# One 96-row load for each of queries, keys and factors, with constant rows below them, and a new list of the work

## The chip, the cores and the metric

The kernel runs on one core of a Trainium2 chip. The metric is the time of one execution on the device, in microseconds. A core has five engines that run side by side, each through its own list of instructions in order: PE (matrix products), VectorE (DVE in the profile), ScalarE (ACT), GpSimd (POOL) and SyncE (SP), which here issues nearly all transfers. An engine waits where an instruction needs what another engine or a transfer has not finished.

## The reference

Two blocks follow each other. The first is a gated linear attention: for each of 4 batches and 8 heads a 48x48 state runs over 768 tokens. Its output, with the heads side by side, is `x` of a second block: a Fourier mix over tokens and channels, a normalisation and two dense layers (384 to 1536 to 384).

```
f = 1.0 / (1.0 + np.exp(-f_logit))
for t in range(S):
    state = f[:, :, t, :, None] * state + np.einsum('bhd,bhe->bhde', k[:, :, t], v[:, :, t])
    y[:, :, t] = np.einsum('bhd,bhde->bhe', q[:, :, t], state)
...
X = np.fft.fft(x, axis=1)
X = np.fft.fft(X, axis=2)
u = x + np.real(X)
un = (u - mu) / np.sqrt(var + 1e-06)
return u + np.maximum(un @ w_ch1, 0.0) @ w_ch2
```

## The kernel before

**Units.** Two heads of one batch make a unit; there are 16 units, four to a batch. A unit's queries, keys and factors (`f_logit`) lie with channels on partitions and tokens along the row, 112 partitions in all: head 0 at 0 to 47, head 1 at 64 to 111. The 16 partitions between, 48 to 63, hold a copy of some rows so that vector work can run over all 112 at once; `FILL` takes in these rows where 64 outputs are wanted, `ROWS` leaves them out. The source rows of both heads follow each other, so `load` (lines 197 to 213) writes 96 rows to partitions 0 to 95 (line 212), which holds head 0, then the first 16 rows of head 1 as filling, then head 1's last 32 rows, and with a second transfer (line 213) 16 rows to partitions 96 to 111, so that 64 to 111 hold head 1 whole. Values come in two transfers (lines 206 and 207).

**Steps of a unit** (`attention`, then `outputs` and `fold`), one for each time that its number stands in the list: 1 exponential and logarithm of the factors on ScalarE (lines 372, 373); 2 a running sum on VectorE (379, 380); 3 exponentials of the sum on ScalarE (383, 384, 387); 4 queries and keys multiplied by them on VectorE (391, 392); 5 products of keys and queries in blocks of 64 tokens on PE (400); 6 their causal mask on VectorE (404); 7 first products with the values and the far blocks (559, 576, 579); 8 the rest of these and the state increments `ds` (599); 9 the state's running sum on VectorE (607); 10 products of states and queries (616) and copies out of PSUM (625 to 629); 11 the turn to tokens on partitions (636, 640, 641); 12 and 13 the folding for the Fourier transform (663 to 687). `K` with a unit's number turns its keys (538, 540).

**The other block.** `F` steps through the Fourier mix of a batch, `H` through its normalisation, `P` through the two dense layers. For batch 0 the first layer is plain products (`up`, line 865) and the first pair of token blocks also has a plain second layer (`po`, line 874). All later ones use fast matrix schemes with fewer products (lines 836 to 845 and 888 to 922), which need sums of weight blocks (`B`, `W`). The dense weights arrive as 64-bit floats in 24 pieces (`r` fetches one, `R` three) and are turned into 32-bit ones (`C`, lines 281 to 285: one step on ScalarE, two on VectorE, one on GpSimd). `V` and `c` read all of them again for a check. `D` is a group of eight matmuls whose result nobody reads (line 192).

**Order.** `ORDER` (line 27) is a list of such words; the loop over it (line 951 on) records each step, and every engine runs its part of the steps in the order recorded, SP's transfers too. A buffer that is loaded again makes SP wait until its last reader is done, and everything behind on SP waits with it. There are two to four buffers each for factors, keys and queries: units 2 and 3 use parts of the large tile `wide_t`, which from unit 8 on serves other ends. A transfer also waits for one that was issued eight before it. Unit 0's first use in the list:

```
"Z I D L0f 0 i D L2f 2 D L1f D 1 L0q 0 L0k r D D D L1q 1 0 D D L0v L1k 0 L2q 2 C D 0 0 L2k 1 D D r 0 "
```

`L0f` loads unit 0's factors, `L3fk` the factors and keys of unit 3, `0` takes unit 0's next step, `i` loads an identity matrix, `Z` and `I` set constants on GpSimd, `T` and `S` load and sort tables of cosines and sines.

Of the kernel before, what the change touches and what calls it, by code (L numbers as in the profile page):

```python
# [12 lines left out]
C = 128  # L13
# [2 lines left out]
HIGH = 22.0  # L16
SMALLEST = 1.125 * 2.0 ** -15
WARM = 2.0 ** 57
X_MIN = -24.0


# [3 lines left out]


ORDER = (
    "Z I D L0f 0 i D L2f 2 D L1f D 1 L0q 0 L0k r D D D L1q 1 0 D D L0v L1k 0 L2q 2 C D 0 0 L2k 1 D D r 0 "
    "L3fk K0 D 1 1 K1 1 C 0 0 r 2 2 L1v D 3 D D r L3q 0 L2v L4fk 3 K2 C 1 0 C 1 1 3 2 1 D 2 3 3 4 2 0 L3v "
    "1 2 L5fk 5 D D 3 4 R 2 1 5 2 3 K3 C 4 3 L4qv 3 T D 2 L6fk 3 L5qv 5 C 4 D 2 4 4 3 3 4 S 2 3 C 5 K4 4 "  # L30
    "F0 F0 4 F0 F0 r C K5 5 6 r C 4 L6qv 5 F0 r r 4 5 L7fk H0 H0 r 5 H0 C 6 C 5 P0 7 P0 P0 r 6 C L7qv 6 "
    "P0 P0 5 C 6 K6 P0 r 6 7 C r P0 C P0 r r 7 C P0 F0 6 5 7 r r L9fk B C P0 P0 6 C 6 r r K7 C F0 P0 7 C "
    "7 C r 6 r H0 r C P0 P0 C 7 6 C P0 L8fk 7 H0 B L8qv 9 P0 P0 H0 B B 9 P0 8 7 P0 B 8 P0 9 B P0 P0 P0 8 "
    "P0 7 L9qv 4 9 9 K9 P0 B P0 5 8 P0 P0 7 H0 9 P0 7 9 8 B 9 H0 6 P0 P0 L11fk 9 11 W P0 6 P0 P0 9 K8 P0 "
    "P0 P0 B P0 P0 P0 P0 P0 8 7 P0 P0 P0 F1 P0 F1 L11qv P0 F1 F1 11 8 F1 P0 8 8 L10fk 10 P0 P0 P0 8 10 H1 "
    "P0 L10qv B P0 11 P0 P0 10 10 H1 B P0 P0 11 10 K10 P0 10 B 10 11 K11 11 L12fk B P0 H1 B B P1 P1 P1 P1 "
    "P1 B P1 P1 P1 P0 P1 P1 P1 P1 F1 P1 P1 F1 P1 P1 10 12 9 12 10 P1 P1 10 8 L12qv H1 9 P1 P1 12 12 10 P1 "
    "P1 H1 11 P1 12 11 H1 12 11 P1 P1 P1 H1 P1 P1 P1 P1 L13fk 13 P1 11 H1 P1 P1 P1 P1 P1 P1 P1 8 P1 P1 12 "
    "K12 L14fk 13 P1 14 P1 P1 12 L13qv 13 11 10 P1 13 12 10 P1 K13 11 P1 P1 P1 P1 P1 P1 14 P1 12 P1 11 P1 "
    "P1 P1 F2 F2 P1 14 P1 L14qv 14 F2 P1 P1 F2 P1 13 13 F2 13 K14 F2 F2 L15fk 13 13 P1 14 13 H2 P1 15 P1 "  # L40
    "15 P1 P1 L15qv 15 14 P1 14 P1 H2 14 15 H2 14 P1 P2 P2 P2 P2 H2 P2 P2 P2 P2 P2 P2 P2 P2 P2 P2 P2 13 "
    "14 15 H2 15 V 13 P2 K15 15 14 15 H2 V 14 15 P2 V P2 14 15 12 P2 P2 P2 15 12 c P2 H2 V P2 P2 P2 P2 P2 "
    "c 15 15 P2 P2 F3 F3 F3 P2 F3 P2 H2 P2 c P2 F3 P2 P2 F3 P2 c V F3 P2 P2 V P2 P2 P2 c c V V P2 P2 P2 "
    "H3 c P2 H3 P2 P2 P2 c P2 H3 P2 P2 P2 P2 P2 P2 P2 P2 V P2 P2 V P2 P2 P2 P2 V P2 P2 P2 c P2 c V c P2 V "
    "P3 c V P2 P3 P3 H3 V H3 P3 P3 P3 P3 P3 H3 P3 P3 P3 P3 P3 P3 P3 c V c c P3 c P3 V V P3 P3 P3 c P3 P3 "
    "P3 P3 P3 V P3 P3 H3 P3 P3 P3 P3 c c P3 V V V P3 P3 V P3 P3 P3 c c P3 P3 P3 P3 P3 P3 c V P3 P3 H3 c "
    "P3 c P3 P3 P3 M P3 P3 P3 P3 P3 P3 P3 P3 P3 P3 P3 P3 P3 P3 P3 P3 P3 P3 P3 P3"
)


# [33 lines left out]
def kernel(  # L84
# [13 lines left out]
    nc = tc.nc  # L98
    B, HP, _, D, _, S = qkf.shape
# [6 lines left out]
    HD = DM // 2  # L106
    QS, QD = S // 4, DM // 4
    R = 64 + D
    ROWS = [slice(64 * r, 64 * r + D) for r in range(2)]

    FILL = [slice(0, 64), slice(64, 64 + D)]

    PLACES = [slice(0, C), slice(2 * C, 3 * C), slice(C, 2 * C)]

# [18 lines left out]
    wide_t = fixed([128, 5 * S + 4], "wide")  # L133
# [33 lines left out]

    place = const.tile([128, B, 4], U32, tag="place", name="place")

    def start():  # L170

        for t in g_t:
            nc.gpsimd.memset(t[:, S:], 0.0)
        nc.gpsimd.memset(bound, HIGH)
        nc.gpsimd.memset(bound.rearrange("p (c t) -> p c t", t=C)[:, :, 0:1], LOW)
        nc.gpsimd.memset(low, LOW)
        nc.gpsimd.memset(eps, 1e-6)
        nc.gpsimd.memset(two, 2.0)
        for t in te_t:
            nc.gpsimd.memset(t, 0.0)  # L180
        nc.gpsimd.memset(causal, 1.0)
        for s in range(2):
            half = causal[64 * s:64 * s + 64, :64]
            nc.gpsimd.affine_select(out=half, in_=half, pattern=[[1, 64]], compare_op=ALU.is_ge, fill=0.0,
                                    base=0, channel_multiplier=-1)

    started = []

# [9 lines left out]
    def load(u, *names):  # L198
        if u >= B * HP:
            return  # L200
        b, hp = divmod(u, HP)
        for name in names:
            if name == "v":
                v_of[u] = (p3.tile([128, NCH, 2 * D], F32, tag="v", name=f"v{u}"),
                           pr.tile([128, NCH // 2, 2 * D], F32, tag="vx", name=f"vx{u}"))
                nc.sync.dma_start(out=v_of[u][0], in_=v[b, hp])
                nc.sync.dma_start(out=v_of[u][1][64:], in_=v[b, hp, :64, 3:])
                continue
            t, i = home(name, u), "qkf".index(name)
            rows = qkf.rearrange("b h r d i s -> (b h r d) i s")  # L210
            first = 2 * D * u
            nc.sync.dma_start(out=t[:2 * D, :S], in_=rows[first:first + 2 * D, i])
            nc.sync.dma_start(out=t[2 * D:R, :S], in_=rows[first + D:first + 64, i])

    def tables():

# [316 lines left out]
    kT_of = {}  # L533
# [8 lines left out]
    def outputs(u, x_all, AT, Q, K, te, T=None):  # L542
# [12 lines left out]
        def values(c, r, rows, t, weights, moved=False):  # L555
            g, o, vals = into(c, r), (c % 3 if moved else c) * 2 * D + r * D, vxf if moved else vf
            new = (c // 3, g) not in opened
            opened.add((c // 3, g))
            nc.tensor.matmul(y[FILL[g], c // 3, c % 3 * C + t.start:c % 3 * C + t.stop],  # L559
                             lhsT=vals[rows, o:o + (64 if g == 0 else D)], rhs=weights,  # L560
                             start=new, stop=True, skip_group_check=True)

# [32 lines left out]
        for c in range(NCH - 1):  # L595
            for r in range(2):

                n = 1 if c < NCH - 2 else 2
                nc.tensor.matmul(ds[FILL[r], :, c:c + n], lhsT=kT_of[u][:, c, FILL[r]],  # L599
                                 rhs=vt[:, c, r * D:(r + 1) * D].unsqueeze(2).to_broadcast([128, D, n]),  # L600
                                 start=True, stop=True)
        yield
# [10 lines left out]
        yield  # L613

        for c, r in ((1, 0), (4, 1), (4, 0), (1, 1), (2, 0), (3, 1), (3, 0), (2, 1), (5, 0), (5, 1)):
            nc.tensor.matmul(y[ROWS[into(c, r)], c // 3, c % 3 * C:c % 3 * C + C], lhsT=st[ROWS[r], :, c - 1],  # L616
                             rhs=Q[ROWS[r], c * C:(c + 1) * C], start=False, stop=True,
                             skip_group_check=True)

# [330 lines left out]
    with tc.manual_schedule():  # L950
        for word in ORDER.split():
            kind, n = word[0], int("0" + "".join(c for c in word if c.isdigit()))
            if kind.isdigit():
                if n not in units:
                    units[n] = attention(n, lambda b=n // HP: x_all(b))
                next(units[n], None)
            elif kind == "K":
                keys_turned(n, home("f", n)[:R, :S])
            elif kind == "F":
                if n not in fronts:  # L960
                    fronts[n], rest[n] = fnet(n, x_of[n]), projected(n, x_of.pop(n))
                next(fronts[n], None)
            elif kind == "P":
                next(rest[n], None)
            elif kind == "W":
                combine()
            elif kind == "B":
                weight_sum()
            elif kind == "H":
                next(behind[n], None)  # L970
            elif kind == "r":
                fetch()
            elif kind == "V":
                reread()
            elif kind == "D":
                busy()
            elif kind == "C":
                weights()
            elif kind == "c":
                sizes()  # L980
            elif kind == "R":
                fetch(3)
            elif kind == "L":
                load(n, *word.strip("L0123456789"))
            elif kind == "I":
                start()
            elif kind == "i":
                nc.sync.dma_start(out=ident, in_=ident_in)
            elif kind == "T":
                wave = tables()  # L990
            elif kind == "S":
                sort_tables(wave)
            elif kind == "Z":
                zeros()
            elif kind == "M":
                flag = judge()
# [3 lines left out]
    with tc.If(again > 0):  # L1000
# [5 lines left out]
                nc.sync.dma_start(out=dst, in_=src[:, cols])  # L1006
        combine()
        nc.sync.dma_start(out=causal.rearrange("p (i n) -> p i n", n=32), in_=sel)
        for u in range(4):
            load(u, *("fkqv" if u < 3 else "qv"))  # L1010
        for b in range(B):
# [77 lines left out]
```

## Time and profile before

| | us |
|---|---|
| median of 3 runs | 530.24 (527.37 to 530.46) |
| the profiled execution | 528.67 |
| its span, first to last instruction | 526.9 |
| PE busy | 497.4 |
| VectorE busy | 379.6 |
| ScalarE busy | 224.8 |
| the `D` matmuls in PE's time | 14.4 |

The profile is of one execution. The span lies 1.8 us below its time, and the execution 1.6 us below the median. The groups of instructions give busy time, the mean of one in ns, and the idle time of the engine just before, with what ended it. Instructions on PE overlap, so its busy time doesn't mean that it runs at its peak. Slices are 13.2 us each.

### The profile page before, as it was taken

What the parts mean: (1) busy time and instruction counts of PE and PEld (TensorE: products, weight loads), DVE (VectorE), ACT (ScalarE), POOL (GpSimd) and SP (SyncE); (2) the same over time, 40 slices, a digit from 0 to 9 for tenths busy, and PEclk for the clock granted to TensorE, in tenths of its full rate; (3) what the DMA queues carried; (4) which work ended last, traced back from release to release, by engine and by line L of the source; (5) the groups of instructions that cost most, each with busy time, mean ns of one, the idle gap of its engine ahead of it and who ended that gap; (6) DMA issues with size and microseconds to landing.
All of it is one profiled execution on the core that took longest, in us unless ns stands there. A gap on an engine that the chain in (4) does not pass through costs nothing.

```text
span 526.9 us, 13784 instructions
## 1 busy us (share of the span) xinstructions
PE 497.4 (94%) x5854; PEld 456.9 (87%) x5854; DVE 379.6 (72%) x746; ACT 224.8 (43%) x529; POOL 58.0 (11%) x85
## 2 busy tenths in 40 slices
PE   4867789999999999999999999999999999999995
PEld 4756668866899889999999889999899999999995
DVE  3777998998896258696598886686787566757561
ACT  6474667655530371444634534451441405132230
POOL 3110633351001000100001000000000000010000
PEclk9788899999999999999999999999999999999998
DMA  8998635674021121103031212110323112421101
GB/s 212 258 242 214 188 106 159 193 214 124 12 76 63 39 70 44 43 1 117 23 89 51 55 55 71 47 63 14 106 61 104 47 61 91 145 66 60 34 1 36
DMA packets 20462, 48.15 MB, mean 91 GB/s; under 512 B 3366, under 2 KB 5991, under 8 KB 20391
## 3 DMA queue, kind: packets, MB, share of 16 engines
q1 hardware_dynamic: 19142, 43.43, 29.5%
q0 software_dynamic: 1104, 3.54, 1.8%
q8 instruction: 48, 0.79, 0.6%
q14 instruction: 24, 0.19, 0.1%
q10 hardware_dynamic: 144, 0.20, 0.1%
HBM read 42.44 MB, written 4.72 MB: 89 GB/s over the span
## 4 chain that ended last, share of the span: by engine, by line
PE 81%; DVE 9%; issue 1%; ACT 1%; DVEq 0%
PE ub L836 24%; PE fx L888 16%; PE fz L888 12%; PE up L865 7%; PE z L725 3%; PE po L874 3%; PE y L559 3%; PE mix L744 2%; PE pt L783 2%; PE ds L599 2%; DVE w L284 2%; PE y L616 2%; PE yt L636 1%; PE sc L400 1%; PE st L538 1%
## 5 line engine op out<-in xcount | busy, mean ns | idle before, releaser
L843 DVE TENSOR_TENSOR h<-h,ub 128x512 f32<-128x512 f32 x81 | 55.1, 686 | 40.4 <-PE ub L836 40.3
L692 POOL DMA_INDIRECT out_dram<-x,place x16 | 17.8, 1112 | 383.5 <-DVE x L918 261.6
L841 ACT ACTIVATE h<-ub 128x512 f32<-128x512 f32 x54 | 32.2, 597 | 58.6 <-PE ub L836 58.1
L865 PE MATMUL up<-unT,w 128*128 128x256 f32 x216 | 49.3, 381 | 0.6 <-ACT unT L784 0.6
L845 ACT ACTIVATE h<-h 128x512 f32<-128x512 f32 x54 | 33.9, 631 | 33.3 <-DVE h L843 33.3
L888 PE MATMUL fx<-block,h 128*128 128x192 f32 x264 | 46.6, 327 | 0.0
L836 PE MATMUL ub<-unT,w 128*128 128x128 f32 x360 | 46.6, 280 | 0.0
L865 PEld LDWEIGHTS up<-unT,w 128*128 128x128 f32 x216 | 40.2, 190 | 6.3 <-ACT unT L784 0.8
L888 PE MATMUL fx<-w,h 128*128 128x192 f32 x264 | 45.4, 327 | 0.0
L836 PEld LDWEIGHTS ub<-unT,w 128*128 128x128 f32 x360 | 43.2, 191 | 0.7
L888 PEld LDWEIGHTS fx<-block,h 128*128 128x128 f32 x264 | 43.3, 190 | 0.1
L888 PEld LDWEIGHTS fx<-w,h 128*128 128x128 f32 x264 | 42.7, 190 | 0.3 <-ACT unT L784 0.2
L836 PE MATMUL ub<-wide 128*128 128x128 f32 x288 | 39.0, 281 | 0.0
L836 PE MATMUL ub<-wide,w 128*128 128x128 f32 x288 | 38.2, 280 | 0.0
L285 POOL TENSOR_TENSOR w<-w,raw 128x384 uint32<-128x384 uint32 x24 | 27.2, 1132 | 75.9 <-DVE w L284 39.1
L836 PEld LDWEIGHTS ub<-wide 128*128 128x128 f32 x288 | 34.6, 191 | 1.0 <-issue 0.4
L836 PEld LDWEIGHTS ub<-wide,w 128*128 128x128 f32 x288 | 34.3, 191 | 1.1 <-DVE h L843 0.3
L379 DVE TENSOR_TENSOR_SCAN W<-g,bound 112x768 f32<-112x768 f32 x12 | 21.0, 1750 | 9.2 <-ACT g L373 9.2
L784 ACT COPY unT<-pt 128x384 f32<-128x384 f32 x24 | 11.6, 487 | 35.8 <-PE pt L783 35.8
L867 ACT ACTIVATE h<-up 128x256 f32<-128x256 f32 x36 | 13.5, 380 | 30.3 <-PE up L865 30.3
L559 PE MATMUL y<-at,v 64*48 64x64 f32 (+1 forms) x768 | 19.3, 229 | 6.6 <-DVE at L404 2.9
L559 PEld LDWEIGHTS y<-at,v 64*64 64x64 f32 (+1 forms) x768 | 15.6, 135 | 10.3 <-issue 4.1
(188 smaller groups left out, 1003.0 us busy)
## 6 DMA issues: line engine op xcount, KB each, us to landing
raw<-in_w_ch_dram SPq DMA_DIRECT2D x24, 384.0 KB, 6.1
v<-in_v_dram SPq DMA_DIRECT2D x16, 288.0 KB, 4.5
k<-in_w_ch_dram SPq DMA_DIRECT2D x12, 384.0 KB, 3.7
g<-in_w_ch_dram SPq DMA_DIRECT2D x12, 384.0 KB, 3.4
k<-in_qkf_dram SPq DMA_DIRECT2D x14, 288.0 KB, 4.0
g<-in_qkf_dram SPq DMA_DIRECT2D x12, 288.0 KB, 6.4
q<-in_qkf_dram SPq DMA_DIRECT2D x12, 288.0 KB
wide<-in_qkf_dram SPq DMA_DIRECT2D x10, 288.0 KB, 5.4
```

What stands on the lines that cost most here:

```text
L285: nc.gpsimd.tensor_tensor(bits, bits, lo, ALU.add)
L379: nc.vector.tensor_tensor_scan(W, g, bound[:R], 0.0, ALU.add, ALU.min)
L559: nc.tensor.matmul(y[FILL[g], c // 3, c % 3 * C + t.start:c % 3 * C + t.stop], lhsT=vals[rows, o:o + (64 if g == 0 else D)], rhs=weights, ...
L692: nc.gpsimd.indirect_dma_start(out=out.rearrange("b s d -> (b s) d"), out_offset=bass.IndirectOffsetOnAxis(ap=place[:, b, i:i + 1], axis=0 ...
L725: nc.tensor.matmul(z[:, cols], lhsT=src[:, j, lo:hi], rhs=tab[:, t, T % 2, cols], start=(i == 0), stop=(i == len(parts) - 1), skip_group_c ...
L836: nc.tensor.matmul(banks[bank][:, m * 128:(m + 1) * 128], lhsT=block(w)[:, m * 128:(m + 1) * 128], rhs=tokens(a), start=(new and m == 0), ...
L841: nc.scalar.activation(out, got, AF.Copy, scale=1.0 if how == "=+" else -1.0)
L843: nc.vector.tensor_tensor(out, out, got, ALU.add if how == "+" else ALU.subtract)
L845: nc.scalar.activation(out, out, AF.Relu)
L865: nc.tensor.matmul(pp[:, :256], lhsT=w1[:, kt, m * 128:(m + 1) * 128], rhs=unT[:, kt], start=(kt == 0), stop=(kt == 2))
L874: nc.tensor.matmul(po[:, :DM], lhsT=h[:, m, t], rhs=w2[:, m], start=(m == 0), stop=(m == NF - 1))
L888: nc.tensor.matmul(out, lhsT=h[:, m], rhs=blocks[i][:, m], start=(start and m == 0), stop=(m == H - 1), skip_group_check=True)
```

## The change

There are two parts. **Rows.** The loads write all 96 rows in one transfer to partitions 16 to 111: head 0 at 16 to 63, head 1 at 64 to 111 as before. Partitions 0 to 15 get constants once: 40 in the factors, 2 to the 19th in the keys, 0 in the queries. With these, head 0's products take in partitions 0 to 63. Matrix products with the states still write 48 rows from 0 or 64 (`OUT`). The constants are set on VectorE for the plain tiles and on GpSimd for those in `wide_t`, in `idle_factors` at the end of `start`, and in `idle_rest` where the list has the new word `E`. **List.** `ORDER` is replaced as a whole. It has the same words in the same numbers, plus `E`; their places differ throughout. Below is its beginning; the rest goes on in the same manner.

```diff
+FULL = 40.0
+IDLE_KEY = 2.0 ** 19
...
-    "Z I D L0f 0 i D L2f 2 D L1f D 1 L0q 0 L0k r D D D L1q 1 0 D D L0v L1k 0 L2q 2 C D 0 0 L2k 1 D D r 0 "
-    "L3fk K0 D 1 1 K1 1 C 0 0 r 2 2 L1v D 3 D D r L3q 0 L2v L4fk 3 K2 C 1 0 C 1 1 3 2 1 D 2 3 3 4 2 0 L3v "
-    "1 2 L5fk 5 D D 3 4 R 2 1 5 2 3 K3 C 4 3 L4qv 3 T D 2 L6fk 3 L5qv 5 C 4 D 2 4 4 3 3 4 S 2 3 C 5 K4 4 "
-    "F0 F0 4 F0 F0 r C K5 5 6 r C 4 L6qv 5 F0 r r 4 5 L7fk H0 H0 r 5 H0 C 6 C 5 P0 7 P0 P0 r 6 C L7qv 6 "
...
+    "Z I L0f L1v D L1f 0 r 1 L2v L0q L0k D E D L1q 0 0 D D 1 L1k r D D D 0 i L2f D 0 L0v L3fk C D 1 0 1 2 "
+    "K0 0 D 2 3 D C L4fk 0 4 L2q 1 L2k D D D 0 L3q D 2 1 2 0 r 4 3 L4qv K1 T S C 1 0 1 L5fk 2 1 3 1 r 2 0 "
+    "K2 3 2 L3v 1 2 C 3 3 L6fk 5 2 D 1 4 D D 4 2 R K3 3 2 3 6 5 3 4 2 L7fk L6qv D C L5qv 3 4 3 4 r C 3 K4 "
+    "2 5 3 4 5 C F0 F0 F0 F0 4 C D r r C F0 4 K5 5 r H0 5 H0 r 5 4 H0 7 5 P0 C L8qv r P0 L7qv 6 7 5 6 P0 "
...
-    ROWS = [slice(64 * r, 64 * r + D) for r in range(2)]
-
-    FILL = [slice(0, 64), slice(64, 64 + D)]
+    IDLE = 64 - D
+    ROWS = [slice(0, 64), slice(64, R)]
+    OUT = [slice(64 * r, 64 * r + D) for r in range(2)]
...
+    def idle_factors():
+
+        for t in g_t[:2]:
+            nc.vector.memset(t[:IDLE, :S], FULL)
+        nc.gpsimd.memset(wide_t[:IDLE, :2 * S + 1], FULL)
+
+    def idle_rest():
+
+        for t, value in ((k_t[0], IDLE_KEY), (q_t[0], 0.0), (k_t[1], IDLE_KEY), (q_t[1], 0.0)):
+            nc.vector.memset(t[:IDLE, :S], value)
+        for t, value in ((k_t[2], IDLE_KEY), (wide_t[:, 3 * S + 2:5 * S + 2], 0.0)):
+            nc.gpsimd.memset(t[:IDLE], value)
...
-            nc.sync.dma_start(out=t[:2 * D, :S], in_=rows[first:first + 2 * D, i])
-            nc.sync.dma_start(out=t[2 * D:R, :S], in_=rows[first + D:first + 64, i])
+            nc.sync.dma_start(out=t[IDLE:R, :S], in_=rows[first:first + 2 * D, i])
...
-            nc.tensor.matmul(y[ROWS[into(c, r)], c // 3, c % 3 * C:c % 3 * C + C], lhsT=st[ROWS[r], :, c - 1],
+            nc.tensor.matmul(y[OUT[into(c, r)], c // 3, c % 3 * C:c % 3 * C + C], lhsT=st[ROWS[r], :, c - 1],
```

## The prediction

> **What bounds the kernel now.** I read the page's first two parts, then a table of busy time by stage, then the waits of each engine in the early stages, and last the DMA issues. PE is the busiest engine, and its row in the 40 slices shows where it is not:
>
> ```profile
> PE 497.4 (94%) x5854; PEld 456.9 (87%) x5854; DVE 379.6 (72%) x746; ACT 224.8 (43%) x529; POOL 58.0 (11%) x85
> PE   4867789999999999999999999999999999999995
> PEclk9788899999999999999999999999999999999998
> DMA  8998635674021121103031212110323112421101
> ```
>
> PE is full from the seventh slice to the last but one. What can be won lies in the first 130 us or the last slice. I cut the span at the first `up` matmul (82.2) and at the end of the first pair's output projection (128.8); columns are length, then busy time per engine, granted clock, DMA share, GB/s.
>
> ```profile
> 6.20:52.40 46.20, 34.05 (x853) 29.85 (x854) 33.54 (x50) 27.37 (x58) 4.05 (x4) 0.85 0.98 241
> 52.40:82.20 29.80, 24.11 (x509) 19.32 (x498) 27.50 (x56) 18.55 (x56) 13.82 (x21) 0.94 0.51 147
> 82.20:128.80 46.60, 45.77 (x533) 34.90 (x534) 42.97 (x65) 30.67 (x71) 17.48 (x15) 1.00 0.63 183
> 128.80:520.00 391.20, 391.18 (x3962) 370.82 (x3961) 275.02 (x577) 145.13 (x342) 17.39 (x16) 1.00 0.19 58
> ```
>
> To 52.4 the DMA engines are full (0.98, 241 GB/s) while VectorE idles 46.2 - 33.5 = 12.7 us. From 52.4 to 82.2 VectorE is the bound (27.5 of 29.8). From 82.2 PE lacks 0.8 us in 46.6, with VectorE close behind (43.0), and from 128.8 nothing is missing in 391 us. So a microsecond gained before 82 shortens the end if VectorE keeps up to 128.8; one gained after that, off PE, is worth nothing. VectorE's and PE's early waits:
>
> ```profile
> DVE W L379 <- ACT g L373: 8.9, 2, 6.2
> DVE stt L607 <- PE ds L599: 5.9, 4, 2.9
> DVE at L404 <- PE sc L400: 2.6, 2, 2.3
> PE ds L599 <- issue: 2.0, 1, 2.0
> PE y L559 <- issue: 2.0, 1, 2.0
> ```
>
> The scan waits for ScalarE, which waits for factors; the state scan waits for PE, which itself stood still twice for 2.0 us with nothing to wait for.
>
> **What the Trainium skill says.** "DMA: Bandwidth & Descriptors", on a DMA's semaphore and its engine count, says a 96-partition tile is spread over all 16 engines; the 0.98 share agrees. "SBUF — State Buffer", who interferes with whom, says a DVE instruction with at most one SBUF input outside the two-port modes doesn't contend with GpSimd, so memsets on both may run side by side; no run here shows it. "VectorE: DVE Perf Modes", on zero memsets, gives one cycle per element; no DVE memset is in this trace. "Runtime: NRT & Kernel Launch", instruction fetch mechanics, calls the crossing of a code block "mostly hidden"; the two pauses of 2.0 us, both with the DMA full, speak for an exception, though the trace doesn't name their cause.
>
> **The change part by part.**
>
> *Loads.* Each of the 48 query, key and factor loads loses its second transfer of 16 rows:
>
> ```profile
> k<-in_qkf_dram SPq DMA_DIRECT2D x14, 48.0 KB, 6.0
> g<-in_qkf_dram SPq DMA_DIRECT2D x12, 48.0 KB, 3.3
> q<-in_qkf_dram SPq DMA_DIRECT2D x12, 48.0 KB, 3.0
> wide<-in_qkf_dram SPq DMA_DIRECT2D x10, 48.0 KB, 4.7
> ```
>
> That is 48 x 48 KB = 2.3 of 48.15 MB, and 48 issues of 0.42 us on SP. Only transfers in the full stretch can count: 19 of them are issued before 50 us, 19 x 49,152 B = 0.93 MB, and / 241 GB/s = **3.9 us of queue time**. The other 29 lie where the DMA engines are busy 0.51 or less on average after a short peak: nothing, hidden by PE. SP's issues run ahead of need (its waits reach 17 us for buffers while PE stays full): nothing. Whether the saved bytes become saved time depends on what follows.
>
> *Constant rows.* VectorE gets six memsets of 16x768, first on its list. At a cycle per element the estimate by the skill's page is 0.8 us each, as against 0.96 for a 112x768 product in this trace: 4.8 us, from 0.8 to 5.6. Bounds: half of that, and 0.96 each, 6.6. VectorE's first scan starts at 6.23, so they cost 0; at the upper bound the first scan slips 0.4. GpSimd gets 1537 + 768 + 1536 elements in three memsets behind `start`; 768 elements took it 0.70 us (1.41 for two), so 3.5 us, ending near 9.5. Its next work was at 17.9, and the first reader of these rows is unit 2's factor step, in the new list after about 19. Nothing, unless they were slowed more than three times. Head 0's products take 64 rows instead of 48 by the same columns; an `at` product with 64 rows takes 228 to 231 ns: nothing.
>
> *New list, first loads.* Values of units 1 and 2 now go ahead of unit 0's queries and keys; unit 2's factors go back. With 4.2 us to the first arrival's lag and 241 GB/s: unit 1's factors are 936 KB deep and land at 8.2; unit 0's keys 2,256 KB, 13.8 (before 1,744 KB, 11.6, but then used only at 13.85 because ScalarE had unit 2's factors first). So the first scores start at 14.8 against 14.86: no gain. Unit 0's values land 3,928 KB deep at 20.9, and PE's first `y` slips from 18.66 to 20.9. Unit 4's factors wait on SP until PE has done with unit 0's (about 21.5), land near 25, and hold ScalarE, in order, before unit 2's exponentials, 26.7 against 24.8. Both delays lie ahead of work that was later still.
>
> Walking both lists on VectorE with the durations of the groups (scan 1.93 with its sum, products 1.93 a pair, mask 1.03, state scan 0.75, fold 2.5): the old one has unit 0 folded and unit 3 scaled at 41.7, with four weight conversions and four scans done. The new one reaches this at about 40.5 with three conversions and five scans. A scan is 1.9, a conversion 0.39 + 0.82 = 1.2, so the **lead is 1.2 + 1.9 - 1.2 = 1.9 us**. Beyond, the old list idles another 2.9 us (one of PE's pauses); later unit values there are nearer, and I credit 1 us of it. Bounds for all before 82: loss of 2 (the pauses of PE return at worse points) to gain of 8 (3.9 of queue time and most of the waits).
>
> *New list, conversions.* Before the first `up` stand 9 weight conversions instead of 11: VectorE reaches it 2 x 1.2 = 2.4 us sooner. They are paid between it and the end of the first pair: 15 conversions instead of 13, on top of 43.0 us busy: 45.4, against PE's 45.8. VectorE becomes almost the bound there, and I give back 1.6.
>
> *The body.* The number of warming groups (21), products and folds is the same; PE stays full in the middle, so reordering is worth nothing there, and can only cost.
>
> **Sum:** -1.9 - 1.0 - 2.4 + 1.6 = -3.7 us, rounded to -3.5 since the walk can't resolve less. The profiled execution took 528.67, its span 526.9, so I expect a span of 523.4. The median of the runs is 530.24, 1.6 above the profiled one; the forecast against it is **526.7 us**.
>
> **Rivals.**
>
> *The whole head moves up (gain of 7 to 9).* If VectorE's 12.7 us of waiting is all due to the full DMA queue, the 3.9 us come through, the pauses of PE shrink with the load, and the conversions' 2.4 us are kept: 522. For it: the DMA share of 0.98. Against: of VectorE's waits only 0.6 us name a DMA; the rest name ScalarE and PE.
>
> *A load held behind another on SP (slower).* In the body each buffer is reloaded just before use; SP issues in order, and ScalarE runs in order. A factor load queued behind a query load whose buffer PE still reads arrives late; ScalarE stands, evictions stop, and PE halts once its two banks are full, after about two product steps (2 x 1.95 us). The place is units 10 to 14, where in the new list unit 13's queries and values go ahead of its factors. A load lands in 4 to 6 us, so each case costs PE 0 to 4; three of them, 12 less the 3.5 gained, give 538. It decides once ScalarE waits longer than 3.9 us. Against: the old list has the same adjacency and PE lost nothing.
>
> *No effect of the loads.* If the queue is limited by rows or by the source and not by bytes, or port use at partitions 16 to 111 is worse, the 3.9 us are not there, and the list alone gives 529 to 531.
>
> **How the numbers follow.** About 1% (5.3 us) is what can be told from no change. Forecast case 0.42 (523 to 530), head moves up 0.25 (518 to 524), slower rival 0.23 (534 to 545), no effect 0.10. Nearly all of the second, with a little of the first, gives 0.29 faster; most of the third and none of the fourth gives 0.22 slower; 0.49 the same. The range 519 to 537 leaves out the ends of the two outer cases.
>
> **What would show it.** DMA full for some 4 us less; the first `up` near 77 to 79 us; between it and the first pair's last projection VectorE busy over 45 us; PE without idle time from 130 on; six VectorE memsets ended by 6.2. Wrong: the first `up` at 82 or later, or PE idle time over 2 us after 130.

## The result and the profile after

| | before | after |
|---|---|---|
| median | 530.35 (4 runs, 527.37 to 533.09) | 1560.27 (4 runs, 1555.43 to 1563.72) |
| ratio, 95% interval | | 2.942 (2.923 to 2.961) |
| span of the profiled execution | 526.9 | 1562.0 |

The kernel takes three times as long. Neither the forecast nor a rival has anything of this size. In the experiments below, one of the 20 executions of e5, two of the 18 of e10 and one of the kernel before ran in a slower state, and their times are left out of all numbers. The page of the kernel after, its first line, engine totals, slices (39 us each now) and three of its groups:

```profile
span 1562.0 us, 37472 instructions
PE 1166.7 (75%) x16518; PEld 1040.0 (67%) x16518; DVE 855.2 (55%) x1686; ACT 464.6 (30%) x1089; POOL 290.1 (19%) x339
...
PE   7799999999999502355898354899355899455898
PEclk8899999999999855555899556899566899555899
...
L880 PE MATMUL up<-unT,w 128*128 128x256 f32 x1080 | 251.7, 394 | 8.0 <-ACT unT L799 6.8
...
L707 POOL DMA_INDIRECT out_dram<-again,place x16 | 16.2, 1015 | 499.0 <-DVE again L933 283.8
...
L707 POOL DMA_INDIRECT out_dram<-x,place x16 | 16.5, 1034 | 385.3 <-DVE x L933 227.8
```

PE has 16518 matmuls where it had 5854, and `up`, the plain first layer, comes 1080 times instead of 216. The output is stored twice, once from `x` and once from a tile `again`. PE's row of slices shows two parts: thirteen and a half full slices, then four groups that look alike, one for each batch. So this is not the old work running slower; work was added behind it. The view of VectorE in order of time has the seam:

```profile
529.76 0.56 DVE L937 TENSOR_TENSOR x<-fx,x 128x384 f32<-128x384 f32 x1 [1.59 <-PE fx L903]
530.91 1.50 DVE L175 MEMSET g<- 16x768 f32 x2 [0.59 <-DVE x L937]
```

The first pass ends with the last addition at 530.3 us (before: 521.3), and at 530.91 the constant rows are set again. This is a branch at the end of the kernel. The kernel guards the range of its numbers: a tile `deep` collects, for each unit and chunk, factor plus running sum (line 395), and where one reaches `HIGH`, 22, a flag makes the core compute everything again in small blocks with plain products.

```
T = deep[:R, u]
nc.vector.tensor_tensor(T, home("f", u)[:R, C::C], W[:, C - 1::C], ALU.add)
...
nc.vector.scalar_tensor_tensor(most[:R], part[:R, 0:1], HIGH, most[:R], ALU.is_ge, ALU.max)
...
again = nc.values_load(flag[0:1, 0:1], min_val=0, max_val=1)
with tc.If(again > 0):
```

The slice `C::C` ends at column 768, one behind the 768 tokens. `start` puts 0 there, on all partitions (line 188). For units 2 and 6 the factor tile is the front of `wide_t`, and the new memset on GpSimd, in order of time on that engine, is this one:

```profile
5.96 1.37 POOL L176 MEMSET wide<- 16x1537 f32 x1
```

1537 is twice 768 and one more: the column between the two tiles is filled too, with 40. The running sum in these rows stays at `LOW`, -10, so the guard reads 40 - 10 = 30, which is over 22. Whether that is the cause was the first thing to test.

Below the large fact lies a small one. The first pass alone ends 9.0 us later than the kernel before. By stage (length, busy time of PE, its weight loads, VectorE, ScalarE and GpSimd, granted clock, DMA share, GB/s), in the cuts of the prediction:

```profile
6.20:52.40 46.20, 33.19 (x769) 28.91 (x768) 31.02 (x46) 27.74 (x56) 12.79 (x23) 0.80 0.84 224
52.40:82.20 29.80, 24.30 (x501) 18.79 (x499) 26.82 (x55) 16.64 (x52) 5.88 (x5) 0.91 0.52 145
82.20:128.80 46.60, 42.19 (x589) 33.02 (x584) 38.73 (x62) 32.79 (x77) 18.99 (x15) 0.96 0.59 165
128.80:520.00 391.20, 390.91 (x3934) 366.58 (x3933) 276.57 (x576) 144.82 (x342) 15.58 (x15) 1.00 0.18 56
```

Behind 128.8 PE is full as before. Ahead of it VectorE does less in each stage than in the kernel before (31.0 against 33.5, 26.8 against 27.5, 38.7 against 43.0), and the DMA share of the first stage is 0.84 instead of 0.98. The loads became lighter, and the work still fell behind.

### The profile page after: what moved, and what is told of

Read it like the earlier page. It is cut to its first block, busy times and chain, and to the rows that moved or that the text cites. A ratio compares the mean times of both kernels' runs of the same rounds, so it can differ in the third digit from the quotient of the medians.

```text
span 1562.0 us, 37472 instructions
## 1 busy us (share of the span) xinstructions
PE 1166.7 (75%) x16518; PEld 1040.0 (67%) x16518; DVE 855.2 (55%) x1686; ACT 464.6 (30%) x1089; POOL 290.1 (19%) x339
## 4 chain that ended last, share of the span: by engine, by line
PE 60%; DVE 15%; POOL 8%; issue 5%; ACT 4%; DMA 0%; POOLq 0%; ACTq 0%; DVEq 0%
PE up L880 15%; PE fx L903 11%; PE fz L903 8%; PE ub L851 8%; PE y L574 4%; PE z L740 3%; POOL w L463 2%; POOL tl L497 2%; PE sd L538 1%; PE yt L651 1%; PE st L553 1%; POOL w L311 1%; PE y L631 1%; PE ds L614 1%; PE mix L759 1%
## 5 line engine op out<-in xcount | busy, mean ns | idle before, releaser
L880 PE MATMUL up<-unT,w 128*128 128x256 f32 x1080 | 251.7, 394 | 8.0 <-ACT unT L799 6.8
L880 PEld LDWEIGHTS up<-unT,w 128*128 128x128 f32 x1080 | 210.9, 198 | 42.6 <-ACT unT L799 10.0
L882 ACT ACTIVATE h<-up 128x256 f32<-128x256 f32 x180 | 68.8, 383 | 173.4 <-PE up L880 173.4
L707 POOL DMA_INDIRECT out_dram<-again,place x16 | 16.2, 1015 | 499.0 <-DVE again L933 283.8
L903 PE MATMUL fx<-block,h 128*128 128x192 f32 x552 | 97.6, 327 | 0.0
L903 PE MATMUL fx<-w,h 128*128 128x192 f32 x552 | 94.5, 326 | 0.0
L574 PE MATMUL y<-at,v 64*48 64x64 f32 (+3 forms) x1152 | 68.3, 293 | 20.3 <-issue 16.5
L574 PEld LDWEIGHTS y<-at,v 64*48 64x48 f32 (+3 forms) x1152 | 52.7, 158 | 31.6 <-issue 26.5
L856 ACT ACTIVATE h<-ub 128x512 f32<-128x512 f32 x54 | 32.2, 597 | 69.0 <-PE ub L851 51.5
L903 PE MATMUL fz<-block,h 128*128 128x192 f32 x276 | 48.6, 326 | 0.0
L903 PE MATMUL fz<-w,h 128*128 128x192 f32 x276 | 48.6, 326 | 0.0
L903 PE MATMUL fz<-w,s 128*128 128x192 f32 x276 | 48.6, 326 | 0.0
```

What stands on the lines that cost most here:

```text
L574: nc.tensor.matmul(y[ROWS[g], c // 3, c % 3 * C + t.start:c % 3 * C + t.stop], lhsT=vals[rows, o:o + (64 if g == 0 else D)], rhs=weights, ...
L707: nc.gpsimd.indirect_dma_start(out=out.rearrange("b s d -> (b s) d"), out_offset=bass.IndirectOffsetOnAxis(ap=place[:, b, i:i + 1], axis=0 ...
L856: nc.scalar.activation(out, got, AF.Copy, scale=1.0 if how == "=+" else -1.0)
L880: nc.tensor.matmul(pp[:, :256], lhsT=w1[:, kt, m * 128:(m + 1) * 128], rhs=unT[:, kt], start=(kt == 0), stop=(kt == 2))
L882: nc.scalar.activation(h[:, m].rearrange("p t n -> p (t n)"), pp[:, :256], AF.Relu)
L903: nc.tensor.matmul(out, lhsT=h[:, m], rhs=blocks[i][:, m], start=(start and m == 0), stop=(m == H - 1), skip_group_check=True)
```

## The experiments

Time is compared with the kernel before in runs taken beside it. "First `up`" is the start of the first plain product of the dense layer, "pair" the end of the last `po` of the first pair of token blocks, both of the profiled execution; behind the pair, 392 to 393 us follow to the end of the last addition in every kernel.

### Does the guard trip on that column?

e1 fills the two tiles and leaves the column between them alone:

```diff
-        nc.gpsimd.memset(wide_t[:IDLE, :2 * S + 1], FULL)
+        for i in range(2):
+            nc.gpsimd.memset(wide_t[:IDLE, i * (S + 1):i * (S + 1) + S], FULL)
```

> The changed kernel, with the constant 40 written to the two factor tiles in wide_t one by one, so that the extra column behind unit 2's factors keeps its zero. Theory (that one column makes the guard true: 40 - 10 = 30, at or over the bound of 22): no second pass, one list only, and since the first pass of the changed kernel ended its last VectorE step at 529.8 us against 520.7 before, a span near 536 and a ratio near 1.017. Rival A (the new list breaks the check of the weights, or the rows' running sums trip the guard): still about 1560 us. Rival B (the first pass ran late only because of the second pass's code behind it): about 527.

Measured: 537.19 us (5 runs), ratio 1.013 (1.007 to 1.018), 5854 matmuls, one pass. That removes the second pass, and it leaves a kernel that is slower than before. e2 and e3 keep the memset of 1537 and change only its constant, to both sides of 22 + 10 = 32:

```diff
-FULL = 40.0
+FULL = 31.5     # e2
+FULL = 32.5     # e3
```

> The changed kernel with the constant for the factors 31.5 instead of 40, nothing else. Theory: 31.5 - 10 = 21.5 stays under the bound of 22, so no second pass: about 536 us, though the column is still wrong. Rival A: about 1560 us, as neither the weights' check nor the running sums of rows with such factors change.

> The same with 32.5. Theory: 32.5 - 10 = 22.5 is over the bound: about 1560 us, while 31.5 gave about 536. Rival A: the same time as with 31.5, whichever it is.

Each of e2, e3 and e4 ran once. The first line of the page of e2, and of e3:

```profile
span 532.9 us, 13720 instructions
```

```profile
span 1554.9 us, 37472 instructions
```

A constant that differs by 1.0 makes a thousand us of difference (534.58 and 1556.65 us), at the place that 22 and -10 give. e4 takes the kernel before and puts 40 into the same column:

```diff
+        nc.gpsimd.memset(wide_t[:16, S:S + 1], 40.0)
```

> The kernel before with 40 written to the extra column behind unit 2's factors in 16 rows; that column enters the guard alone. Theory: the second pass runs, so about 530 + 1028 = 1558 us, and the whole loss of the changed kernel is the price of that pass, whatever the rows and the list. Rival A: 530 us, if the guard does not look at that column.

```profile
span 1543.5 us, 37622 instructions
```

It took 1545.2 us, 13 below the expectation, but with the same second pass. So the column alone does it, with the old loads and the old list too: the cause is shown from both sides. The second pass costs 1545 - 530 = 1015 us here, and 1557 - 535 = 1022 between e3 and e2.

### Rows and list apart

e5 has the new rows (with e1's memsets) and the old list, plus the word `E`; e6 the old rows and the new list without `E`:

```diff
-    "Z I L0f L1v D L1f 0 r 1 L2v L0q L0k D E D L1q ..."
+    "Z I E D L0f 0 i D L2f 2 D L1f D 1 L0q 0 L0k r ..."
```

> The new rows with the old list (its word E right behind I) and the column put right. Theory L (the list costs the remaining 7 us, the rows gain a little): 525 to 530 us, ratio 0.99 to 1.00. Rival R (the rows cost, by one larger transfer at partitions 16 to 111 or by the memsets): 534 to 538 us.

> The new list on the kernel before, with its two transfers a load and no constant rows. Theory L: slower than before, 537 to 542 us, since more bytes and more transfers stand in the same queue. Rival R: near 530 us.

| | time | ratio, 95% interval |
|---|---|---|
| new rows, old list (e5) | 528.40 (19 runs) | 0.998 (0.996 to 1.000) |
| old rows, new list (e6) | 542.37 (4 runs) | 1.024 (1.019 to 1.029) |
| both (e1) | 537.19 (5 runs) | 1.013 (1.007 to 1.018) |

The list costs 8 to 13 us. The rows give 5 us with the new list; with the old one 1 us, which the interval doesn't tell from nothing. The profile of e5 shows where the rest may have gone. From 6.2 to 52.4 us its DMA share is 0.88 against 0.98, 4.6 us of the stage, but its first `up` starts at 82.4, as before (82.2). PE's view in order of time has a pause there for which the trace names no releaser:

```profile
29.98 0.23 PE L209 MATMUL y<-bound 128*128 128x128 bf16 x1 [3.77 <-issue]
```

VectorE's state scan then waits 6.1 us for PE. The kernel before had two such pauses of 2.0 us. So the bytes were saved, and this execution stood in a longer pause instead. What the pause is, no run tested.

### The queue at the tables

e1's VectorE waits ahead of the first `up`, the three longest (total, number, longest):

```profile
DVE w L299 <- DMA raw<-in_w_ch_dram: 6.8, 1, 6.8
DVE stt L623 <- PE ds L615: 4.8, 2, 2.6
DVE W L395 <- ACT wide L389: 4.3, 2, 3.0
```

The first line stands for one wait, for the fourth piece of dense weights. In the kernel after it is the same, here VectorE and then SP's issues in order of time:

```profile
39.85 0.96 DVE L407 TENSOR_TENSOR wide<-W,k 112x768 f32<-112x768 f32 x1
47.15 1.05 DVE L298 TENSOR_SCALAR w<-raw 128x384 uint32<-128x384 uint32 x1 [6.34 <-DMA raw<-in_w_ch_dram]
```

```profile
33.75 0.27 SPq L247 DMA_DIRECT2D wave<-in_dim_tab_dram  x1
...
37.29 0.37 SPq L325 DMA_DIRECT2D raw<-in_w_ch_dram  x1
```

The piece is issued at 37.3 behind all the tables, whose words the new list moves ahead of that fetch; a mask and a state scan stand behind the conversion on VectorE, and PE's state products behind the scan. One table, at 33.75, has 97 rows. The Trainium skill ("DMA: Bandwidth & Descriptors", on why a DMA raises its semaphore by 16) says that a transfer is spread over the largest number of engines up to 16 that divides its rows, so 97 rows, a prime, go to one. At a sixteenth of the 241 GB/s measured early in the kernel before, the estimate for its 149 KB is 9.9 us; the trace has 9.7, from issue at 33.75 to the reader's start at 43.4, and e1, e7 and e9 have 9.6 to 10.2 for the same table. A weight piece that is spread over all engines would then wait for its share on this one; e8 tests that. e7 puts the fetch ahead of the tables; e8 loads the table as 96 rows and 1:

```diff
-L4qv K1 T S C 1 0 1 L5fk 2 1 3 1 r 2 0     # e7
+L4qv K1 r T S C 1 0 1 L5fk 2 1 3 1 2 0
...
-nc.sync.dma_start(out=wave[0][0:QD + 1], in_=dim_tab[0:QD + 1, 0])     # e8
+nc.sync.dma_start(out=wave[0][0:QD], in_=dim_tab[0:QD, 0])
+nc.sync.dma_start(out=wave[0][QD:QD + 1], in_=dim_tab[QD:QD + 1, 0])
```

> e1 with the fetch of the fourth weight piece moved in the list from behind the tables and unit 5's factors to ahead of the tables. In the changed kernel this piece was issued at 37.3 us, behind the 97-row table at 33.8, and VectorE stood 6.3 us for it. Theory Q (that transfer in front of it is what VectorE waits for): VectorE's wait goes, 531 to 533 us. Rival S (SP is held by buffers that PE has not freed, or the DMA engines are simply full): the next load is as late, at most 1 us gained, 536 us or more.

> e1 with the 97-row table transfer cut into 96 rows and 1 row. Theory Q in its strong form (97 rows do not divide over the engines, so one DMA engine carries 149 KB alone for some 9.7 us, and each later transfer waits for its share on that engine): the table lands within about 3 us of the transfers ahead, the weight piece lands about 6 us sooner, 530 to 532 us, as in e7 or better. Rival S: no change, 536 to 538 us.

Measured: 536.15 us, ratio 1.014 (1.009 to 1.018), and 535.82, 1.012 (1.006 to 1.018). In the profiles each edit does its part: in e7 no wait for a weight piece is left ahead of the first `up`, and in e8 the longest is 3.4 us, with the table read 4.0 us after its issue (33.3 to 37.3) instead of 9.7; the first `up` comes at 83.6 and 82.2 instead of 88.8. But the timed runs move by 1.0 and 1.4 us, less than the intervals, and both miss the 530 to 533 us expected. Part of the gap is the choice of execution: the profiled one of e1 is the slowest of its five (540.75), that of e7 the fastest, and the kernel after, with e1's list, has its first `up` at 85.2. And in both the pair ends 50 to 52 us after the first `up`, where the kernel before takes 46.7: something is lost behind the first `up` too.

### The two halves of the list exchanged

Up to the first `P0`, old and new list have issued nearly the same steps, so the halves can be joined: e9 is the new list up to there, then `C C 5 6`, then the old list; e10 the old one, then the new; e12 is e9 with the edits of e7 and e8; e11 is e5 with the edit of e8. (The "third weight fetch" in e12's expectation is the fourth piece's, as in e7.)

```diff
-    "... r H0 5 H0 r 5 4 H0 7 5 P0 C L8qv r P0 L7qv 6 7 5 6 P0 ..."
+    "... r H0 5 H0 r 5 4 H0 7 5 C C 5 6 P0 P0 P0 r 6 C L7qv 6 P0 P0 5 C 6 K6 ..."     # e9
```

> The long loads and the constant rows with the two separate memsets, and a list made of two: the new list up to its first P0, then C C 5 6 so that the same steps have been issued as in the old list at this place, and from there the old list. If the new list loses mainly before the first up matmul (tables ahead of the weight piece, walk wrong from 40.5 us on): most of the loss stays, the first up at 87 to 90 us (two conversions more ahead of it than in the new list), and the end of the first pair's projection some 46 to 47 us later, 134 to 136; time 533 to 536 against 530. If it loses mainly between the first up and the end of the first pair: 529 to 531.

> The same loads and memsets with the halves the other way round: the old list up to its first P0, and from there the new list, less the two conversions and the two attention steps that were already issued. If the order after the first up loses 4 to 5 us by itself: first up near 82.4 and the end of the first pair's projection 50 to 52 us later, 133 to 134; time 532 to 534. If that stretch was long only because the new head hands it fewer conversions and later weight pieces: 46 to 47 us, time 528 to 530.

> The long loads and constant rows with two separate memsets, the old list, and the sort table loaded as 96 rows and 1 row. If the 97-row transfer holds VectorE or PE up with the old list too, up to 2 us shorter than without the split: 526.5 to 528 against 529.4 before. If with the old list nothing waits for the table or for the weight piece behind it: 528.5 to 529.5, a ratio within 0.3% of 1.

> The new head with the third weight fetch ahead of the tables and the sort table split in 96 rows and 1 row, then C C 5 6 and the old list. If the queue at the tables is what the new head loses by, and the 3.5 us of lead forecast for the list exist without it: first up (after two conversions more) at 80 to 82 and time 526 to 528. If the new head is late by other waits too (for scores, for the factors of units 3 and 4): first up 84 to 86, time 530 to 533.

| list: head, rest | first `up` | pair | between | ratio, 95% interval |
|---|---|---|---|---|
| old, old (before) | 82.2 | 128.9 | 46.7 | |
| old, old (e5) | 82.4 | 129.6 | 47.2 | 0.998 (0.996 to 1.000) |
| old, old, split table (e11) | 80.8 | 128.3 | 47.5 | 1.000 (0.998 to 1.002) |
| new, old (e9) | 87.0 | 133.9 | 46.9 | 1.007 (1.005 to 1.009) |
| new, old, fetch and split (e12) | 79.7 | 128.0 | 48.3 | 1.000 (0.998 to 1.003) |
| old, new (e10) | 79.0 | 130.3 | 51.3 | 1.012 (1.009 to 1.014) |
| new, new (after) | 85.2 | 137.7 | 52.5 | |
| new, new (e1) | 88.8 | 140.3 | 51.5 | 1.013 (1.007 to 1.018) |
| new, new, old rows (e6) | 93.6 | 144.0 | 50.4 | 1.024 (1.019 to 1.029) |

The column "between" sorts by the rest alone: 46.7 to 48.3 with the old rest, 50.0 to 52.5 with the new one (e7 and e8 among them), whatever head and rows. The new rest loses 2 to 6 us, 4 in the middle of both groups. The timed runs agree: 1.2% with the old head (e10 against e11) and 0.6% with the new one (e1 against e9).

The column "first `up`" is less firm. The same head gives 85.2, 87.0 and 88.8 (after, e9, e1), the old head with the new rows 79.0 and 82.4 (e10, e5), so one profile fixes it to some 3.6 us. The head's part stands out of that: e9 is 87.0 with the tables in the way, and e12, the same list with the two repairs, 79.7. In the medians, 533.87 against 529.51, it is 4.4 us, well outside the intervals. That e12 comes 2.5 us ahead of the kernel before is within the spread, and its time is the same: what is shown is that the repairs take the head's loss away, not that they leave a gain.

Where the new rest loses can be read from the stage between first `up` and pair, e9 first, then e10 (columns as above):

```profile
87.00:133.90 46.90, 45.90 (x535) 35.12 (x534) 41.79 (x63) 29.90 (x69) 17.49 (x15) 1.00 0.60 175
```

```profile
79.00:130.30 51.30, 46.40 (x536) 34.79 (x536) 42.50 (x70) 32.96 (x74) 18.67 (x15) 1.00 0.50 148
```

PE does the same work, 46 us, and stands for 1.0 in one and 4.9 in the other. (In e1, e8 and the kernel after, PE takes 48 us for it, at a granted clock of 0.97; that is nearly 2 us of their loss.) The longest of PE's waits in e10, VectorE's longest, and SP's issues of weight pieces around it:

```profile
115.39 0.52 PE L799 MATMUL pt<-ident,un 128*128 128x128 f32 x3 [2.67 <-DVE un L796]
```

```profile
105.29 0.36 DVE L299 TENSOR_SCALAR w<-raw 128x384 uint32<-128x384 uint32 x1 [2.79 <-DMA raw<-in_w_ch_dram]
```

```profile
95.94 0.33 SPq L326 DMA_DIRECT2D raw<-in_w_ch_dram  x1
100.34 3.66 SPq L326 DMA_DIRECT2D raw<-in_w_ch_dram  x3
```

PE waits for `un`, the normalised tokens of the next pair, which it turns in `pt`; VectorE stood for weight pieces for 4.8 us in this stage, since SP, with loads of other units between, issued the next piece only at 100.3. e1 has the same three things (4.3 us for pieces, 2.0 for `un`). But these waits alone don't make the loss: e12, with the old rest, stands 3.7 us for pieces and PE idles 1.9; e7, with the new rest, has 3.8 and 3.8. The stage cut at the start of this `pt`, e9 first, then e10, shows what differs:

```profile
87.02:123.36 36.34, 35.34 (x497) 28.59 (x497) 33.36 (x53) 23.61 (x58) 16.68 (x15) 1.00 0.65 191
123.36:133.91 10.55, 10.55 (x37) 6.53 (x38) 8.44 (x11) 6.27 (x11) 0.81 (x1) 1.00 0.43 120
```

```profile
79.00:115.39 36.39, 32.15 (x423) 26.10 (x423) 31.66 (x51) 26.46 (x63) 15.42 (x12) 1.00 0.65 192
115.39:130.33 14.94, 14.28 (x114) 8.72 (x117) 10.84 (x20) 6.50 (x12) 3.25 (x3) 1.00 0.13 41
```

`pt` starts 36.4 us after the first `up` in both. The new rest has put 32 us of PE's work ahead of it instead of 35, so PE arrives early and stands, and 14 us behind it instead of 10.6, which then have to be done. All six profiles with the new rest have 32 us ahead, all others in the table 35 to 36 ahead and 10.6 behind. So the order loses by what it leaves PE to do while VectorE, with its waits for pieces, gets to `un`. This is read from the profiles; no run moved `un` or took the waits for pieces away.

e10 and e12 missed their expectations. e10's first `up` came at 79.0 instead of 82.4, and its median, 535.60, above the 532 to 534 expected. Its 16 runs spread from 529.8 to 537.7, 11 of them at 535 or more, and the profile is of one with 530.4: what the longer executions lose in addition is not shown. e12's time, 529.5, lies between its two cases, and its stage up to the pair is 1.6 us longer than before. e11 was no faster for the split table, as its second case said. No version beat the kernel before by more than its interval.

## Why the prediction was wrong

**The step that failed is "Constant rows".** It counts the memsets on GpSimd as "1537 + 768 + 1536 elements", prices them and closes with "Nothing, unless they were slowed more than three times". The price was right: they took 3.4 us for 3.5 and ended at 9.3 for "near 9.5". But 1537 is one more than two rows, and the step never asked what lies in that column and who reads it. Its readers were taken to be "unit 2's factor step"; the guard at line 395 reads one column further, and its branch, which the kernel before has in its code but never in its trace, costs 1015 us. The view could not show it, since the branch doesn't run there. The rival "No effect of the loads" doubts the bytes alone; one by which the constants change a value that decides on work was missing.

**Loads.** "DMA full for some 4 us less" is right: 4.6 us in e5. "Whether the saved bytes become saved time depends on what follows" decided it: with the old list 1 us of time came, or none, of the 3.9. "No effect of the loads" is near that outcome, but not by its reason, since the bytes did leave the queue. The sum has no term of its own for the 3.9. Two readings were wrong beside it: seven of the other 29 transfers lie between 82 and 129 us, where the share is 0.63 and not "0.51 or less", and only the first of PE's two pauses falls in full queues (1.01; at the second, 44.8 to 46.8 us, it is 0.46).

**VectorE's memsets** ended at 5.77 for 5.6, with 0.70 us each for 0.8, while GpSimd ran memsets of its own, and the first scan started at 6.09: hidden, as said. The estimate of 0.8 us was drawn from the Trainium skill ("VectorE: DVE Perf Modes", on zero memsets: a cycle per element); the trace has 0.70, an eighth less, and decides.

**First loads.** First scores at 14.2 (said 14.8), first `y` at 20.0 (20.9), unit 2's exponentials at 26.7 (26.7): right. So was the walk: unit 3 is scaled at 40.8, said "about 40.5".

**The credit of 1 us beyond the walk** is the second step that failed. It begins where the walk ends, and the very next instruction on VectorE waits 6.3 us. The walk put durations of VectorE one behind the other and did not follow SP's queue, where `T` and `S` had moved ahead of a weight fetch; "SP's issues run ahead of need" was said of the query, key and factor loads and applied to all. "The first `up` near 77 to 79 us" became 85.2, which the prediction itself names as wrong ("at 82 or later"). Whether the lead of 1.9 us exists without that wait is not shown: with both repairs the first `up` comes at 79.7, where the old head has 79.0 to 82.4. The bound of 2 us of loss was too near, since it allowed for PE's pauses alone.

**The conversions** are the third. "2 x 1.2 = 2.4 us sooner" counts what stands ahead of `P0` in the lists, 9 against 11. But the first `up` waits for `un`, and on VectorE the old list's last two conversions stand behind it. The kernel before, in order of time:

```profile
80.51 0.48 DVE L780 TENSOR_SCALAR un<-x,mv,rstd 128x384 f32<-128x384 f32 x1 [1.02 <-ACT rstd L771]
80.90 0.36 DVE L283 TENSOR_SCALAR w<-raw 128x384 uint32<-128x384 uint32 x1
```

Nine stand ahead of it in both kernels, and 14 start between the first `up` and the pair in both, so the 2.4 us were never there to gain. (The two more that the expectations of e9 and e12 count come behind `un` as well.) "I give back 1.6" falls with them: VectorE's busy time in e1's stage is 41.4 us and not 45.4, of 51.5. The loss there, about 4 us, comes from the order of PE's work around `un`, for which the sum has no term.

**The body** was right: "worth nothing there" is 392 to 393 us from the pair to the end of the last addition in all kernels, and PE's idle time after 138 us of the first pass is 0.3 us. The slower rival, a load held behind another on SP, came near by luck: what arrived late were weight pieces between 37 and 120 us and not factors of units 10 to 14, the first of them behind a transfer in the queue and not behind a buffer that PE still read, and VectorE stood, not ScalarE.

## What to carry to other kernels

Where a change writes constants into padding, list every reader of each column it touches, those that only decide on a branch too, and count elements against the shape: one too many is a reader you don't know. When work is moved up, walk the transfer queue as well as the engines, and ask of each transfer that is moved what now stands behind it. Count the work ahead of the very instruction that the next stage waits for, not ahead of the stage's word in a list. A busy share of a queue falls by what a change saves, but the time falls only if the last wait of that stage was for the queue.

## What the runs showed of the hardware

A transfer of 97 rows and 149 KB took 9.6 to 10.2 us from issue to its reader in four kernels; as 96 rows and 1 row it took 4.0 at most (e8), and pieces of 384 KB took 6.2 in the median (e1). A memset of 16x768 on VectorE took 0.70 us. PE paused with no releaser in the trace, and in three kernels with new rows and the old head such a pause near 28 to 30 us goes with the first `up`: 1.6 and 79.0 (e10), 3.0 and 80.8 (e11), 3.8 and 82.4 (e5). The DMA engines were full then (1.04 to 1.06), but the kernel after has a pause of 1.6 us near 43 at a share of 0.28. Whether these are the crossings of a code block that the prediction suspected, the trace doesn't say, and no run tested it.
